# Storing linear-attention features as split parts: the step is moved from the output pairs to the down projection

## The chip, the cores and the metric

The kernel runs on 1 core of a Trainium2 chip. The metric is the device time of one execution in microseconds (us); the time before is the median of three runs. Names of engines follow the profile: PE (TensorE matmul), PEld (its weight loads), DVE (VectorE), ACT (ScalarE), POOL (GpSimd), SP (SyncE, which issues every DMA here).

## The reference

```python
x = A_x                                   # 1 x 2048 x 1024, float32
xn = _layernorm(x, axis=-1)
s = _A_ref(xn, A_wqkv, A_w_phi, A_wo)     # 32 heads of 32, Hedgehog linear attention
g = _silu(_B_ref(xn, B_w_gate, B_w_up, B_w_down))   # (sigmoid(xn Wg) * (xn Wu)) Wd, F = 3584
return x + s * g

# in _A_ref, per head:
pq = q @ w_phi;  pk = k @ w_phi
phi_q = concat(softmax(pq), softmax(-pq));  phi_k = concat(softmax(pk), softmax(-pk))
kv = phi_k^T v;  z = sum over s of phi_k
o = (phi_q kv) / (phi_q z + 1e-6)
return o.reshape(B, S, D) @ wo
```

## The kernel before

Every large product is done in float32 by three TensorE passes: an operand is split into a high part (ACT rounds it to `F32R`) and a low part (DVE subtracts the high part from the source), and `mm3` adds high x high, high x low and low x high (lines 146 to 148). `split` (lines 137 and 138) is the helper for that. On top of it each product is a seven-product Strassen form, with operands named B11, T2, T3, B21, T1, T4, B22.

The stages follow each other: the normalisation and the projections of V, K and Q; the gated products; then the **down stage** (h times `w_down`), and last the **pairs**.

The down stage is a list `dsteps`: for six of the seven operands 14 steps with both token chunks c = 0, 1 (84 steps), then B22 chunk by chunk (28 steps with one chunk). `down_load` issues the DMAs of a step ahead of time (one block of `w_down` or of its sums `wd_d`, and a block of `h_d` for each chunk) into raw half slots from `raw_free`, `down_prep` splits them, one `split` a block, and `mm3` uses them. A tick is one chunk, twelve matmuls. At the end of an operand `evacuate` reads the eight banks out (for B21: a DVE copy, line 1810, and an ACT reload of the bank, line 1811).

In the same ticks `q_late` makes the query features, one unit for each of 16 token tiles t and two halves hb, on a plan of ticks: `weigh` (POOL, line 1005), `density` (DVE, a long reduction and four tiny steps, lines 1010 to 1016), `scale` (POOL, line 1022), `turn` (a DVE transpose, line 1026), `keep` (four DMAs to `et_d`, line 1030). So `et_d` holds the features in float32, divided by the denominator and turned.

The pairs are eight pairs of token tiles. For each, `e_load` (line 1057) fetches the features into slots 47 and 48, one for each q (which half of the k blocks); `phi_part` splits them, `hi` on ACT (line 1070) and `lo` on DVE (line 1072), into the ring `phu`; `numerators` (line 1082, four half-width matmuls) multiplies them by kv; `numerators_out` adds the bank's halves, `cp` on ACT and `ad` on DVE; `o_sum` and `o_part` make the Strassen operands of the next pair; `products` and `product_out` multiply by `wo`; `scaled` (POOL) multiplies by g and adds x; `store` writes the result. `gx_load` fetches g and x.

The order of the pairs is written by hand: `PAIR` is a list of names, and `in_order` ties each engine (PE, DVE, ACT, POOL and SP) to that order. `nm101` means numerators with hb 1, q 0, b 1; `e10` the load for hb 1, q 0; `hi10` and `lo10` its split; `gT20` one k of product T2; `vT2` its read-out; `xT2h` and `xT2l` an operand's split; `m`, `a` the scaling, `l` the load of g and x, `y` the store; `-` and `+` mean the pair before and after. `e` names of hb 1 load for the pair whose numerators run now, `e00+` and `e01+` for the one after. Before the first pair `attend` runs the first numerators between the last steps of the down stage. Elsewhere a scheduler sets the order of the instructions, engine by engine.

Of the kernel before, what the change touches and what calls it, by code (L numbers as in the profile page):

```python
# [50 lines left out]
def hedgehog_glu_kernel(  # L51
# [29 lines left out]
    et_d = dram.tile([TT, 2, P, 2 * HB], F32, name="et_d")  # L81
# [41 lines left out]

    def halves(*ids):
        return [slots[i][:, a] for i in ids for a in range(2)]
# [792 lines left out]

    def down_load():

        n = len(down_loads)
        if nests or len(ops) - 1 not in wraw or n == len(dsteps) or len(raw_free) < 1 + len(dsteps[n][2]):
            return False
        i, j, cs = dsteps[n]
        r, *hr = [raw_free.popleft() for _ in range(1 + len(cs))]
# [3 lines left out]
        down_loads.append((clock[0], r, hr))  # L929
        return True  # L930

    def down_prep():
        n = len(dready)
        if n >= len(down_loads) or not wfree or len(hfree) < len(dsteps[n][2]):
            return False
        at, r, hr = down_loads[n]
        if clock[0] < at + LEAD:
            return False
        w = wfree.popleft()
        split(pair(w), r)  # L940
        hs = {}
# [3 lines left out]
        dready.append((w, hs))  # L945
        for o in (r, *hr):
            down_back(o)
        return True
# [29 lines left out]
    def q_late(at, t, hb):  # L978
# [27 lines left out]

        def density():
            st = hold["sa"] = small.tile([P, 5, 16], F32, name=f"sa{t}{hb}", tag="sa", bufs=2)
            r, d2, r2 = hold["r"], *[st[:, a:a + 2].rearrange("p t h -> p (t h)") for a in (0, 2)]
            nc.vector.tensor_reduce(d2, whole(52).rearrange("p (g d) -> p g d", d=DH), axis=AX.X, op=ALU.add)  # L1010
            nc.vector.tensor_mul(d2, d2, r)
            r, d2, r2 = [a.rearrange("p (b t k) -> p b t k", b=2, t=2) for a in (r, d2, r2)]
            den = st[:, 4].rearrange("p (b k) -> p b k", b=2)
            nc.vector.scalar_tensor_tensor(den, d2[:, :, 0], EPS_DEN, d2[:, :, 1], op0=ALU.add, op1=ALU.add)
            nc.vector.reciprocal(den, den)
            nc.vector.tensor_mul(r2, r, den[:, :, None].to_broadcast([P, 2, 2, 8]))

        def scale():
            e3, r2 = hold["e"].rearrange("p (g d) -> p g d", d=DH), hold["sa"][:, 2:4].rearrange("p t h -> p (t h)")
            for a in range(2):  # L1020
                gs = slice(16 * a, 16 * a + 16)
                nc.gpsimd.tensor_mul(e3[:, gs], e3[:, gs], r2[:, gs, None].to_broadcast([P, 16, DH]))

        def turn():
            hold["et"] = whole(etr.next())
            nc.vector.transpose(hold["et"], hold["e"])

        def keep():
            for c in range(4):
                nc.sync.dma_start(et_d[t, hb, c * DH:(c + 1) * DH].rearrange("f (a x) -> a f x", a=4),  # L1030
                                  hold["et"][:, c * 256:(c + 1) * 256])
# [3 lines left out]
        for n, f in steps + ((11, weigh), (14, density), (15, scale), (18, turn), (18, keep)):  # L1035
            later(at + n, f)
# [7 lines left out]
    phu = Ring((44, 20))  # L1044
# [3 lines left out]
    e_next, units_ph, of = {(u, q): 0 for u in range(2) for q in range(2)}, {}, {}  # L1048
# [5 lines left out]
    def e_load(u, q):  # L1054
        tp_, hb = divmod(e_next[u, q], 2)
        if tp_ < NTP:
            nc.sync.dma_start(slots[47 + q][:, u].rearrange("p (a x) -> p a x", a=4),
                              et_d[2 * tp_ + u, hb].rearrange("p (a q x) -> p q a x", a=4, q=2)[:, q])
        e_next[u, q] += 1

    nbank = {}

    def phi_part(part, hb, q):
        if part == "hi":
            b = run(phu.next(), 2).rearrange("p a b n -> p (a b n)")
            units_ph[hb, q] = b.rearrange("p (a k t) -> p a k t", a=2, t=256)
        hi, lo = [units_ph[hb, q][:, a].rearrange("p k (c t) -> p k c t", t=32) for a in range(2)]
        src = whole(47 + q).rearrange("p (c k t) -> p k c t", k=4, t=32)
        if part == "hi":
            nc.scalar.copy(hi, src)  # L1070
        else:
            nc.vector.tensor_sub(lo, src, hi.bitcast(F32))  # L1072

    def numerators(hb, q, b):

        ph = units_ph[hb, q]
        kg = slots[KVB[hb]][:, q].rearrange("p (k m) -> p k m", m=P)
        nbank[hb, q, b] = ps = nmr.next()
        for j in range(2):
            k = 2 * j + b  # L1080
            for a in range(2):
                nc.tensor.matmul(ps[:, j * 256:(j + 1) * 256], kg[:, k], ph[:, a, k], start=a == 0, stop=a == 1)
# [14 lines left out]

    def o_part(tp_, i, part):
        (b11, b12), (b21, b22) = [(o[:, 0], o[:, 1]) for o in oraw]
        b = {B11: b11, T1: b11, B22: b22, T2: b22, T3: b12, B21: b21, T4: b21}[i]  # L1100
        if tp_ not in of:
            of[tp_] = {j: ofr.next() for j in range(7)}
# [6 lines left out]
    def attend():  # L1109

        def phi(hb, q):
            for part in ("hi", "lo"):
                phi_part(part, hb, q)
            for u in range(2):
                e_load(u, q)
# [5 lines left out]
        def numerator(hb, q):  # L1121
# [4 lines left out]
            if (hb, q) == (0, 1):  # L1126
                of[0] = {i: ofr.next() for i in range(7)}
                o_operand(B11)
                o_sum("s11")
# [6 lines left out]
        for hb in range(2):  # L1136
            ph, nm = [[(f, hb, q) for q in range(2)] for f in (phi, numerator)]

            out += [*ph, *nm]
# [693 lines left out]
    for n, (i, j, cs) in enumerate(dsteps):  # L1833
# [30 lines left out]
        if n == ND - 2 * NJ:  # L1864
            assert len(WO[B21]) == 4
            side.extend([lambda k=k: wo_prep(B21, k) for k in range(4)])
            side.extend([lambda u=u, q=q: e_load(u, q) for q in range(2) for u in range(2)])
        if n == ND - NJ:
# [5 lines left out]
            step(1000)  # L1874
            side.extend([lambda fn=fn, a=a: fn(*a) for fn, *a in attend()])
# [29 lines left out]
    for n in range(2):  # L1905
# [7 lines left out]
        gB110 mT4- xT4h- gB111 vB22- xT4l- gB112 mT1- hi00 gB113 gT20 lo00 aT1- e10 gT21 hi01 aT4- vB11 gT22 lo01 e11 gT23  # L1913
        lB22- gB210 lB21- nm001 cp001 yT1- nm000 yT4- cp000 ad001 gB211 vT2 ad000 gB212 nm011 cp011 ad011 hi10 gB213 mB22-
        nm010 lo10 e00+ w0 w1 aB22- gT30 w2 w3 cp010 ad010 hi11 vB21 gT31 nm101 lT1- yB22- cp101 lo11 e01+ gT32 aB21 ad101
        xB11h nm100 gT33 cp100 yB21 gT10 xB11l nm111 lT4 ad100 s11 cp111 vT3 gT11 nm110 ad111 cp110 xT1h ad110 gT12 xT1l
        gT13 xB22h sA xB21h gT40 vT1 gT41 xB22l xT3h gT42 xB21l sB gT43 xT3l gB220 gB221 sC xT2h gB222 vT4 gB223
        xT2l""".split()
# [70 lines left out]
    def last_weights(k):  # L1989
# [9 lines left out]
        (r"(hi|lo)(\d)(\d)", True, lambda p, part, h, q: phi_part(part, int(h), int(q))),  # L1999
# [6 lines left out]
        (r"e(\d)(\d)", True, lambda p, h, q: [e_load(u, int(q)) for u in range(2) if e_next[u, int(q)] == 2 * p + 2 + int(h)]),  # L2006
# [51 lines left out]
```

## Time and profile before

| what | value |
|---|---|
| median of three runs | 2352.37 us (2348.41 to 2358.05) |
| the profiled execution | 2348.29 us, span 2346.5 us |
| PE busy | 2307.9 us, 98% of the span |
| DVE, ACT, POOL busy | 1750.8, 1231.1, 1153.2 us |
| mean granted TensorE clock | 0.943 |
| DMA | 631.33 MB, 269 GB/s mean |
| stores to `et_d` | 1635.4 to 2054.0 us after the start |
| loads from `et_d` | 1977.9 to 2304.4 us |

A row of the timeline gives start, duration, engine, line, operation and tiles, and in square brackets how long the engine stood idle before it and what ended that. A row of the waits gives the waiting engine and line, the releaser, total us, how often, and the longest. A matmul's duration is modelled and overlaps the next one's, so the distance of starts is what counts. A row of a group gives the busy time, the mean in ns, and the idle time before it. The granted clock is a share of full speed; 0.95 is what the profile shows where PE is busy without a gap.

### The profile page before, as it was taken

Reading aid. Unit: us, or ns where it says so; the run is one execution under the profiler, and the core shown is the slowest. Engines: PE = TensorE matmul, PEld = TensorE weight load, DVE = VectorE, ACT = ScalarE, POOL = GpSimd, SP = SyncE. Lnnn points to the kernel's source line nnn. Section 1 sums busy time; section 2 is a strip of 40 time slices with the busy share of each in tenths; the row PEclk is TensorE's granted clock in tenths of the full one; section 3 lists DMA queues with packets and bytes.
Section 4 is the critical chain, followed back from the end, with each engine's and each line's share of the span. In section 5 each row is a group of like instructions: output and inputs, shape, how many; then the busy total and the mean of one; then the engine's idle time right before and its main releaser. Section 6 shows DMA issues by size and latency. Waiting matters only on the chain.

```text
span 2346.5 us, 32121 instructions
## 1 busy us (share of the span) xinstructions
PE 2307.9 (98%) x10533; PEld 1918.4 (82%) x10533; DVE 1750.8 (75%) x2107; ACT 1231.1 (52%) x1965; POOL 1153.2 (49%) x813
## 2 busy tenths in 40 slices
PE   9999999999999999999999999999989999998988
PEld 8888888888888888888888888888878888877777
DVE  8625777876888774777874665657999999977887
ACT  7354577776555555555555545444444345354543
POOL 1323436772231054665653666764464445424676
PEclk9999999999999999999999999999989999989989
DMA  8789977988778868897886867679767666786665
GB/s 298 267 308 364 333 288 286 354 305 311 273 263 296 274 241 281 302 310 265 286 309 222 293 216 246 224 274 352 255 227 241 232 208 217 268 278 218 197 202 178
DMA packets 344185, 631.33 MB, mean 269 GB/s; under 512 B 37841, under 2 KB 87249, under 8 KB 339409
## 3 DMA queue, kind: packets, MB, share of 16 engines
q1 hardware_dynamic: 344016, 629.28, 77.8%
q8 instruction: 82, 1.34, 0.2%
q14 instruction: 87, 0.70, 0.1%
HBM read 378.34 MB, written 250.81 MB: 268 GB/s over the span
## 4 chain that ended last, share of the span: by engine, by line
PE 85%; DVE 6%; DMA 5%; issue 2%; SPq 1%; ACT 1%; POOL 1%; DVEq 0%; ACTq 0%; POOLq 0%
PE bank L147 27%; PE bank L148 27%; PE bank L146 27%; DMA fc<-g_d 2%; PE bank L381 1%; PE bank L744 1%; DMA fa<-h_d 1%; DVE x L1072 1%; DVE x L1107 1%; DVE fb L1072 1%; DMA et_d<-x 1%; DVE w L138 1%; DMA fa<-w_down 0%; DVE x L138 0%; DMA fc<-et_d 0%
## 5 line engine op out<-in xcount | busy, mean ns | idle before, releaser
L146 PE MATMUL bank<-x,w 128*128 128x512 f32 x2248 | 875.1, 390 | 9.9 <-ACT bank L1811 7.5
L147 PE MATMUL bank<-x,w 128*128 128x512 f32 x2248 | 876.7, 390 | 4.9 <-DVE x L138 4.9
L148 PE MATMUL bank<-x,w 128*128 128x512 f32 x2248 | 875.6, 390 | 0.0
L138 DVE TENSOR_TENSOR w<-fa,w 128x512 fp32r<-128x512 f32 (+2 forms) x394 | 395.0, 1009 | 259.0 <-ACT w L137 246.8
L146 PEld LDWEIGHTS bank<-x,w 128*128 128x128 f32 x2248 | 423.1, 188 | 98.7 <-ACT bank L1811 7.9
L147 PEld LDWEIGHTS bank<-x,w 128*128 128x128 f32 x2248 | 423.2, 188 | 93.0 <-DVE x L138 6.1
L148 PEld LDWEIGHTS bank<-x,w 128*128 128x128 f32 x2248 | 422.9, 188 | 87.9
L137 ACT CAST w<-fa 128x512 fp32r<-128x512 f32 (+2 forms) x394 | 267.9, 684 | 318.9 <-PE bank L147 201.4
L146 PE MATMUL bank<-w,x 128*128 128x512 f32 x708 | 278.3, 393 | 0.0
L148 PE MATMUL bank<-w,x 128*128 128x512 f32 x708 | 276.5, 391 | 0.0
L147 PE MATMUL bank<-w,x 128*128 128x512 f32 x708 | 276.4, 390 | 0.0
L148 PEld LDWEIGHTS bank<-w,x 128*128 128x128 f32 x708 | 133.4, 188 | 28.5 <-DVE x L1256 0.7
L146 PEld LDWEIGHTS bank<-w,x 128*128 128x128 f32 x708 | 133.6, 189 | 26.3
L147 PEld LDWEIGHTS bank<-w,x 128*128 128x128 f32 x708 | 133.7, 189 | 26.2
L138 DVE TENSOR_TENSOR w<-fb,w 128x512 fp32r<-128x512 f32 (+1 forms) x116 | 113.8, 983 | 40.3 <-ACT w L137 40.1
L137 ACT CAST w<-fb 128x512 fp32r<-128x512 f32 (+1 forms) x116 | 70.4, 607 | 108.5 <-PE bank L147 80.8
L138 DVE TENSOR_TENSOR x<-fb,x 128x512 fp32r<-128x512 f32 (+1 forms) x87 | 88.7, 1022 | 19.0 <-ACT x L137 16.0
L1401 ACT COPY fc<-bank 128x512 f32<-128x512 f32 x116 | 66.7, 583 | 39.0 <-PE bank L148 15.6
L138 DVE TENSOR_TENSOR p<-fc,p 128x512 fp32r<-128x512 f32 (+1 forms) x68 | 54.6, 813 | 38.4 <-ACT p L137 38.1
L137 ACT CAST x<-fb 128x512 fp32r<-128x512 f32 (+1 forms) x87 | 65.3, 753 | 12.2 <-DMA fb<-xr_d 5.5
L686 ACT ACTIVATE fc<-fc 128x1024 f32<-128x1024 f32 x44 | 46.6, 1060 | 45.2 <-DVE fc L683 27.5
L1096 POOL TENSOR_TENSOR fc<-fc 128x512 f32<-128x512 f32 x32 | 50.0, 1564 | 40.9 <-DVE fc L1091 15.1
(411 smaller groups left out, 3815.0 us busy)
## 6 DMA issues: line engine op xcount, KB each, us to landing
m_d<-fc SPq DMA_DIRECT2D x168, 256.0 KB
fa<-h_d SPq DMA_DIRECT2D x152, 256.0 KB
fa<-wf_d SPq DMA_DIRECT2D x32, 1024.0 KB
x<-m_d SPq DMA_DIRECT2D x128, 256.0 KB
fa<-w_gu SPq DMA_DIRECT2D x102, 256.0 KB
h_d<-fc SPq DMA_DIRECT2D x102, 256.0 KB
fc<-qkv_d SPq DMA_DIRECT2D x86, 256.0 KB
fb<-w_gu SPq DMA_DIRECT2D x72, 256.0 KB
```

The costliest lines, as they stand in the source:

```text
L137: nc.scalar.copy(o[0], src)
L138: i = nc.vector.tensor_sub(o[1], src, o[0].bitcast(F32))
L146: nc.tensor.matmul(o, a[0], b[0], start=first, stop=False, **kw)
L147: nc.tensor.matmul(o, a[0], b[1], start=False, stop=False, **kw)
L148: last_mm[:] = [nc.tensor.matmul(o, a[1], b[0], start=False, stop=last, **kw).ins]
L381: nc.tensor.matmul(ps[:, gs], r[:, gs], bd[:, 4 * f + g], start=g == 0, stop=g == 3, skip_group_check=True)
L686: nc.scalar.activation(e, e, AF.Exp)
L744: nc.tensor.matmul(kvb[g // 2][:, g % 2 * 256:g % 2 * 256 + 256], v[:, g].rearrange("p a f -> p (a f)"), ph[:, g].rearrange("p a f -> p (a ...
L1072: nc.vector.tensor_sub(lo, src, hi.bitcast(F32))
L1096: nc.gpsimd.tensor_sub(o, a, b)
L1107: nc.vector.tensor_sub(lo, b, hi.bitcast(F32))
L1401: nc.scalar.copy(o, banks[b])
```

## The change

**In the down stage** a unit of features now ends with its split. `density` keeps only the long reduction on DVE; three tiny steps become `denominators` on POOL, the reciprocal stays on DVE as `inverse`, and the last tiny product goes to POOL at the head of `scale`. After `turn` comes `parted`: ACT casts the high part, DVE subtracts in place. `keep` stores both parts, eight DMAs in place of four, and `et_d` is twice as large. Each later step of a unit stands two to five ticks later.

**Down's raw blocks**: where a step has both chunks, `raw_take` finds a whole slot for the two blocks of h, one DMA fetches them and one `split` of 1024 columns a partition makes both.

**In the pairs** `phi_part` and the slots 47 and 48 are gone. `e_load` fetches both parts, four DMAs for a q, into slots 44, 45 (q 0) and 20, 21 (q 1), and the numerators read those slots. There is one such buffer for a q. `PAIR` is written anew, and the operands of the next pair take their slots in another order.

```diff
-        for c, o in zip(cs, hr):
-            nc.sync.dma_start(o, h_d[i, j, :, c])
+        if slot is None:
+            nc.sync.dma_start(hr[0], h_d[i, j, :, cs[0]])
+        else:
+            nc.sync.dma_start(slots[slot], h_d[i, j])
...
-        for c, o in zip(dsteps[n][2], hr):
-            hs[c] = hfree.popleft()
-            last_split[:] = [split(pair(hs[c]), o).ins]
+        if slot is None:
+            i = split(pair(hs[0]), hr[0])
+        else:
+            o = run(hs[0], 2)
+            i = split((o[:, :, 0], o[:, :, 1]), slots[slot])
...
             nc.vector.tensor_reduce(d2, whole(52).rearrange("p (g d) -> p g d", d=DH), axis=AX.X, op=ALU.add)
-            nc.vector.tensor_mul(d2, d2, r)
-            nc.vector.scalar_tensor_tensor(den, d2[:, :, 0], EPS_DEN, d2[:, :, 1], op0=ALU.add, op1=ALU.add)
+        def denominators():
+            r, d2, _, den = parts()
+            nc.gpsimd.tensor_mul(d2, d2, r)
+            nc.gpsimd.tensor_add(den, d2[:, :, 0], d2[:, :, 1])
+            nc.gpsimd.tensor_scalar_add(den, den, EPS_DEN)
+        def inverse():
             nc.vector.reciprocal(den, den)
-            nc.vector.tensor_mul(r2, r, den[:, :, None].to_broadcast([P, 2, 2, 8]))
         def scale():
+            nc.gpsimd.tensor_mul(r2, r, den[:, :, None].to_broadcast([P, 2, 2, 8]))
...
+        def parted():
+            nc.scalar.copy(hold["hi"].bitcast(F32R), hold["lo"])
+            nc.vector.tensor_sub(hold["lo"].bitcast(F32R), hold["lo"], hold["hi"])
...
-        for n, f in steps + ((11, weigh), (14, density), (15, scale), (18, turn), (18, keep)):
+        for n, f in steps + ((11, weigh), (14, density), (15, denominators), (16, inverse), (17, scale), (20, turn),
+                                  (21, parted), (23, keep)):
...
+    def e_load(q):
+        tp_, hb = divmod(e_next[q], 2)
         if tp_ < NTP:
+            for a in range(2):
+                for u in range(2):
+                    o = slots[e_slots[q] + a][:, u].bitcast(F32)
+                    nc.sync.dma_start(o.rearrange("p (a x) -> p a x", a=4),
+                                      et_d[2 * tp_ + u, hb, a].rearrange("p (a q x) -> p q a x", a=4, q=2)[:, q])
+        e_next[q] += 1
...
-                nc.tensor.matmul(ps[:, j * 256:(j + 1) * 256], kg[:, k], ph[:, a, k], start=a == 0, stop=a == 1)
+                nc.tensor.matmul(ps[:, j * 256:(j + 1) * 256], kg[:, k], ph[a][:, :, k], start=a == 0, stop=a == 1)
...
-        gB110 mT4- xT4h- gB111 vB22- xT4l- gB112 mT1- hi00 gB113 gT20 lo00 aT1- e10 gT21 hi01 aT4- vB11 gT22 lo01 e11 gT23
+        gB110 mT1- vB22- aT1- lB22- gB111 nm001 cp001 mT4- gB112 nm000 e10 ad001 cp000 aT4- lB21- yT1- gB113 vB11 gT20 nm011
+        ad000 cp011 mB22- yT4- gT21 nm010 e11 ad011 cp010 aB22- lT1- gT22 ad010 yB22- gT23 xB11h vT2 w0 w1 nm101 xB11l cp101
```

SP in one middle pair, before. `fc<-et_d` are the loads of features (e10 and e11 at first, two DMAs each), `g_d` and `x` the loads of g and x, `out` the stores.

```order
L1057 DMA fc_101<-et_d 128x4x128 x4
L1902 DMA fc_101<-g_d 128x512
L1903 DMA fc_101<-x 128x512
L1902 DMA fc_101<-g_d 128x512
L1903 DMA fc_101<-x 128x512
L1967 DMA out<-fb_0_99 128x512
L1967 DMA out<-p_3_16248 128x512
L1057 DMA fc_101<-et_d 128x4x128 x2
```

The same stretch of SP after. `fb` is the buffer of q 0 (slots 44, 45), `x_4` that of q 1 (slots 20, 21); the first row is e10, the second load row e11.

```order
L1116 DMA fb_15910<-et_d 128x4x128 x4
L1946 DMA fc_101<-g_d 128x512
L1947 DMA fc_101<-x 128x512
L2010 DMA out<-fb_0_99 128x512
L2010 DMA out<-p_3_16224 128x512
L1116 DMA x_4_15908<-et_d 128x4x128 x4
L1946 DMA fc_101<-g_d 128x512
L1947 DMA fc_101<-x 128x512
L2010 DMA out<-fb_0_99 128x512
L1116 DMA fb_15910<-et_d 128x4x128 x4
```

Both e10 and e11 are four DMAs now; between them stand a g and an x load and two stores, which before stood behind both.

PE in the middle of a pair, before: numerators nm001, nm000 on `fb` (the split of q 0), then products, and nm011 on `x_4` (that of q 1).

```order
L1082 MATMUL bank_102<-fb_15942,p_9711 128x256 x4
L1082 MATMUL bank_103<-fb_15942,p_9711 128x256 x4
L146 MATMUL bank_106<-w_95,x_7_15941 128x512
L147 MATMUL bank_106<-w_95,x_7_15941 128x512
L148 MATMUL bank_106<-w_95,x_7_15941 128x512
L146 MATMUL bank_106<-w_95,x_7_15941 128x512
L147 MATMUL bank_106<-w_95,x_7_15941 128x512
L148 MATMUL bank_106<-w_95,x_7_15941 128x512
L1082 MATMUL bank_104<-x_4_15940,p_9711 128x256 x4
```

PE after, from nm010 (the last that reads q 1's first half) to nm101 (the first that reads what e10 fetched).

```order
L1128 MATMUL bank_105<-x_4_15908,p_9711 128x256 x4
L150 MATMUL bank_107<-x_5_11981,fa_16223 128x512
L151 MATMUL bank_107<-x_5_11981,fa_16223 128x512
L152 MATMUL bank_107<-x_5_11981,fa_16223 128x512
L150 MATMUL bank_107<-x_5_11981,fa_16223 128x512
L151 MATMUL bank_107<-x_5_11981,fa_16223 128x512
L152 MATMUL bank_107<-x_5_11981,fa_16223 128x512
L1128 MATMUL bank_102<-fb_15910,p_9711 128x256 x4
```

The numerators moved towards the pair's start: the first two stand behind the products gB111 and gB112 (before: behind gB210), and the two that read what e10 and e11 fetch follow the last reader of the same buffer at a distance of five products and two numerators.

DVE in the down stage, before, around one unit's `density` (L1010 to L1016) with down's splits (L138) between.

```order
L1010 TENSOR_REDUCE sa_13480<-fc_101 128x32
L138 TENSOR_TENSOR x_2_5913<-fa_98,x_2_5913 128x512
L1011 TENSOR_TENSOR sa_13480<-sa_13480,stq_13280 128x32
L1026 STREAM_TRANSPOSE x_3_9793<-x_6_12000 128x1024
L138 TENSOR_TENSOR w_95<-fa_98,w_95 128x512
L1014 SCALAR_TENSOR_TENSOR sa_13480<-sa_13480 128x16
L1015 RECIPROCAL sa_13480<-sa_13480 128x16
L1016 TENSOR_TENSOR sa_13480<-stq_13280,sa_13480 128x32
```

DVE after, one unit's reduction (L1053) and reciprocal (L1063), with another unit's transpose (L1075) and its subtraction of the high part (L1079); a split (L142) of 128x2x512 is one of two blocks.

```order
L1053 TENSOR_REDUCE sa_14458<-fc_101 128x32
L142 TENSOR_TENSOR x_2_5913<-fb_100,x_2_5913 128x512
L142 TENSOR_TENSOR w_95<-fa_98,w_95 128x2x512
L1075 STREAM_TRANSPOSE x_3_9793<-fc_101 128x1024
L695 TENSOR_REDUCE stq_14373<-x_6_11984 128x32
L142 TENSOR_TENSOR x_2_5913<-fb_0_99,x_2_5913 128x512
L1063 RECIPROCAL sa_14458<-sa_14458 128x16
L696 RECIPROCAL stq_14373<-stq_14373 128x32
L1079 TENSOR_TENSOR x_3_9793<-x_3_9793 128x1024
```

The three tiny products are gone from DVE, and the reciprocal stands behind work of POOL.

More of the change, by code (lines that the diff above doesn't have):

```diff
@@ L1047, in hedgehog_glu_kernel @@
     nmr, amm = Ring(banks[:4]), Ring(banks[4:])
[L1048 removed]
+    e_next, of, e_slots = [0, 0], {}, (44, 20)
     oraw = [slots[50], slots[51]]
@@ L1101, in o_part @@
         if tp_ not in of:
-            of[tp_] = {j: ofr.next() for j in range(7)}
+            operands_of(tp_)
         hi, lo = pair(of[tp_][i])
@@ L1126, in numerator @@
             if (hb, q) == (0, 1):
-                of[0] = {i: ofr.next() for i in range(7)}
+                operands_of(0)
                 o_operand(B11)
@@ L1136, in attend @@
         for hb in range(2):
-            ph, nm = [[(f, hb, q) for q in range(2)] for f in (phi, numerator)]
-            out += [*ph, *nm]
+            out += [(int,)] * 6
+            for q in range(2):
+                out += [(numerator, hb, q), (e_load, q)]
         return out
```

111 lines of the change are left out of this document (63 added, 48 removed).

## The prediction

> **What bounds the kernel now.** I read the page first, then the table by windows, PE's waits, and then the chain of waits and the timelines of the last 215 us, where the waits lie.
>
> ```profile
> span 2346.5 us, 32121 instructions
> ...
> PE 2307.9 (98%) x10533; PEld 1918.4 (82%) x10533; DVE 1750.8 (75%) x2107; ACT 1231.1 (52%) x1965; POOL 1153.2 (49%) x813
> ...
> PE 85%; DVE 6%; DMA 5%; issue 2%; SPq 1%; ACT 1%; POOL 1%; DVEq 0%; ACTq 0%; POOLq 0%
> ```
>
> The profiled execution took 2348.3 us, 1.8 beyond its span and 4.1 below the median of the three runs (2352.4). TensorE carries the chain. What can be won is its idle time alone.
>
> ```profile
> 1700.00:1750.00 50.00, 42.53 (x179) 34.69 (x178) 45.57 (x60) 21.70 (x36) 28.33 (x20) 0.89 0.70 232
> 1900.00:1950.00 50.00, 50.00 (x223) 41.39 (x222) 47.41 (x64) 18.72 (x30) 24.33 (x18) 0.95 0.67 211
> 2200.00:2250.00 50.00, 45.09 (x207) 37.47 (x206) 43.72 (x45) 24.25 (x37) 37.36 (x22) 0.89 0.58 187
> ...
> PE bank L1082 <- DVE x L1072: 10.6, 6, 2.4
> PE bank L146 <- ACT bank L1811: 7.5, 1, 7.5
> PE bank L147 <- DVE x L138: 4.9, 3, 2.5
> PE bank L146 <- DMA x<-wo_d: 3.6, 4, 1.3
> ...
> PE bank L1082 <- DVE fb L1072: 2.8, 7, 0.8
> PE bank L146 <- ACT x L137: 2.4, 1, 2.4
> ```
>
> Columns of the windows: length, then PE, PEld, DVE, ACT, POOL busy, granted clock, DMA share, GB/s. At 1900 (down stage) PE has no gap, though DVE is busy for 47.41 of 50. Nearly all waits of PE lie at three places: 7.5 us at 1736 (banks read out at the end of B21), 7.3 at the end of the down stage (L147, L137), and in the pairs, at the numerators (L1082), which wait for the feature split's low part (L1072).
>
> ```profile
> 2029.73 0.39 PE L147 MATMUL bank<-x,w 128*128 128x512 f32 x1
> ...
> 2051.03 0.39 PE L148 MATMUL bank<-x,w 128*128 128x512 f32 x1
> ...
> 2139.68 1.11 PE L1082 MATMUL bank<-fb,p 128*128 128x256 f32 x8
> 2168.01 1.12 PE L1082 MATMUL bank<-fb,p 128*128 128x256 f32 x8
> 2302.99 1.11 PE L1082 MATMUL bank<-fb,p 128*128 128x256 f32 x8
> 2204.26 0.62 PE L1082 MATMUL bank<-x,p 128*128 128x256 f32 x3 [2.22 <-DVE x L1072]
> ...
> 2201.50:2204.91 3.41, 1.19 (x7) 0.84 (x6) 3.20 (x3) 1.18 (x2) 3.33 (x3) 0.95 1.07 333
> 2204.92:2208.33 3.41, 3.41 (x11) 2.85 (x10) 3.29 (x6) 1.68 (x3) 1.71 (x2) 0.50 1.01 327
> 2312.14:2315.55 3.41, 1.79 (x12) 1.55 (x12) 3.32 (x5) 0.58 (x1) 2.78 (x2) 0.95 0.69 216
> 2315.56:2318.96 3.40, 3.40 (x16) 2.63 (x16) 3.34 (x6) 1.88 (x4) 1.86 (x2) 0.95 0.84 283
> ```
>
> 95 matmuls stand from 2029.73 to 2051.03: 0.2266 us each. Eight half-width ones take 1.11 with the last one's modelled 0.28, so 0.12 each. A pair has 84 and 32 of them: 19.0 + 3.8 = 22.9 us. Each pair's first numerators start at 2139.68, 2168.01 (28.3 later) and, five pairs on, at 2302.99: 27.0 each. So 4.1 us of a pair are lost: about 2.5 to waits, and the rest to the clock. The 2.22 us wait left PE 1.19 busy in one 3.41 us window, and the next window ran at 0.50, with 11 matmuls for 16; with 1.79 busy the clock stayed at 0.95.
>
> **The change part by part.** *Pairs, what goes.* Four casts on ACT and four subtractions on DVE (L1070, L1072) leave each pair, so 13.4 us of PE waits (10.6 + 2.8) and their slow windows go. What is late next is the load: a numerator now reads the DMA's own target, one buffer for each q, so the load for the second half (e10, e11) can start only when the first half's numerators are done, and PE waits for it directly. There are four 256 KB loads where there were two.
>
> ```profile
> 2218.92 3.42 SPq L1057 DMA_DIRECT2D fc<-et_d  x4
> 2223.52 5.89 DMA fc<-g_d
> GB/s 0 0 0 0 0 0 0 0 2 170 217 285 266 320 309 309 193 39 164 188 238 295 311 313 285 324 217 193 180 139 66 98 131 98 188 287 344 303 295 328
> ...
> 2097.71 1.20 SPq L1057 DMA_DIRECT2D fc<-et_d  x2
> 2104.12 1.05 ACT L1070 CAST fb<-fc 128x1024 fp32r<-128x1024 f32 x1 [2.88 <-DMA fc<-et_d]
> ```
>
> The GB/s row is 2218 to 2228 in slices of 0.25 us. The first bytes come 1.3 us after the issue at 2218.92, and two loads (0.52 MB) are through by 2222.25: 1.0 us a load. So four land 5.3 us after the first issue in an empty queue at best; in a full one, two needed 6.4 (2097.71 to 2104.12). Only the two loads of lB22 stand shortly ahead of e10, so I take 5.8. Between the last numerator of q=0's first half and the first of its second half, PE has five products and two numerators: 15 x 0.2266 + 8 x 0.12 = 4.4 us. First wait: 1.4 us (ends 0.9 and 4).
>
> e11 stands on SP behind e10, a g and an x load (lB21) and two stores: 12 transfers. At best 1.3 + 8 x 1.0 + 4 x 0.8 (256 KB at 330 GB/s) = 12.5 us after e10's issue. The worst from rows: four loads and three others took from 2218.92 to 2229.41 (the chain's piece, 2223.52 + 5.89), 10.5 us; with one more and four loads, 15.3. PE comes to that numerator after 4.4 + 1.4 + two numerators and three products (3.0) = 8.8. Second wait: 3.7 to 6.5; I take 4.0, near the low end, as the high one holds a lull (the GB/s row's 66 to 139). A wait of 4 us leaves some window under 1.2 us busy, so a slow window follows; it costs (1 - 11/16) x 3.41 = 1.1, less what of it falls into the wait: 1.0 (ends 0 and 1.6). A pair then takes 22.9 + 1.4 + 4.0 + 1.0 = 29.3, +2.3 in each of five. In the first pair there is nothing to store or fetch between e10 and e11, so the second wait is 1.3 + 8.0 - 8.8 = 0.5; and the loads w0 to w3 now stand ahead of e00, so the 3.6 us for wo_d go: 24.8 for 28.3, -3.5. The last stretch, from 2302.99 on: 1.6 of waits go (the window at 2312.14), 6.4 come: +4.8. Sum for the pairs 11.5 - 3.5 + 4.8 = +12.8 (ends -3 and +30).
>
> The numerators' right operand is now read in pieces of 32 columns, 128 apart. No matmul here shows that: between nothing and twice 0.12 x 32, or +3.8 a pair. ACT's cast at 2104.12 read the same tile in the same pieces, 1.05 us for 1024 columns, so I take nothing.
>
> The Trainium skill (TensorE: Matmul & The Clock Gate, What's actually happening) lets the clock fall after at least one idle window of about 3.4 us; by that a 4 us wait seldom fills an aligned window, and the sum would be 6 us lower. The trace differs: a 2.22 us wait was enough.
>
> *End of the down stage.*
>
> ```profile
> 2062.05 1.04 ACT L1070 CAST x<-fc 128x1024 fp32r<-128x1024 f32 x1 [9.45 <-DMA fb<-w_down]
> 2064.98:2068.38 3.40, 0.92 (x3) 0.51 (x3) 3.40 (x3) 3.40 (x8) 2.95 (x3) 0.50 0.76 236
> ```
>
> ACT stood 9.45 us before a feature cast, with down's splits queued behind; that made PE's 4.9 and 2.4 and about 2.5 more at clock 0.50. The cast is gone, and PE itself waits for the loads at the first numerators, in a full queue, for 0 to 10: -5 (ends -9 and +2).
>
> *Down stage.*
>
> ```profile
> L138 DVE TENSOR_TENSOR w<-fa,w 128x512 fp32r<-128x512 f32 x131 | 121.6, 936 | 19.1 <-ACT w L137 17.8 <-issue 1.0 <-PE bank L148 0.3
> L1011 DVE TENSOR_TENSOR sa<-sa,stq 128x32 f32<-128x32 f32 x20 | 16.2, 809 | 0.0
> L1014 DVE SCALAR_TENSOR_TENSOR sa<-sa 128x16 f32<-128x16 f32 x32 | 11.5, 360 | 0.4
> L1016 DVE TENSOR_TENSOR sa<-stq,sa 128x32 f32<-128x32 f32 x20 | 6.0, 298 | 0.5
> L138 DVE TENSOR_TENSOR w<-fa,w 128x1024 fp32r<-128x1024 f32 x66 | 92.0, 1401 | 86.2 <-ACT w L137 86.0
> L534 POOL TENSOR_TENSOR fa<-fa 128x256 f32<-128x256 f32 x7 | 5.2, 738 | 50.3 <-DMA fa<-wg_d 46.4 <-DVE bank L1579 3.9
> 1705.85 0.68 DVE L138 TENSOR_TENSOR w<-fb,w 128x512 fp32r<-128x512 f32 x1
> 1706.44 1.78 DVE L138 TENSOR_TENSOR x<-fb,x 128x512 fp32r<-128x512 f32 x1
> 1718.24 1.25 DVE L1026 STREAM_TRANSPOSE x<-x 128x1024 f32<-128x1024 f32 x1 [3.21 <-POOL x L1022]
> 1736.27 0.79 PE L146 MATMUL bank<-x,w 128*128 128x512 f32 x1 [7.47 <-ACT bank L1811]
> L1030 SPq DMA_DIRECT2D et_d<-x x128: 503/514/1444, 1635.4 to 2054.0; - x128
> ```
>
> DVE: the tiny steps leave, 32 x (0.81 + 0.36 + 0.30) = -47 us; 84 block pairs split as one, 84 x (1.40 - 2 x 0.94) = -40; 32 feature subtractions come, x 1.40 = +45. Together -42: DVE gets room, but PE has no gap there, so 0. ACT gains 32 casts of 1.05 and loses 84 starts; it is busy for 18.7 to 21.7 of 50. POOL gets 128 tiny steps: from nothing to the 0.74 of the smallest row, and up to 1.1 of waiting for DVE (a split takes 1.78 beside POOL, 0.68 alone); at 0.6 each 77 us in the 419 us from 1635.4 to 2054.0, so some 35 of 50 busy. A unit's chain now crosses between DVE and POOL twice more, and DVE stands in order (3.21 at the transpose). Splits queue behind, and PE behind them; cover is the splits made ahead. +1 (0 to +12). SP: 128 more stores x 0.51, or +66 us of issue in those 419, less 84 loads, and 16.8 MB more to write beside a DMA share of 0.67; the loads are issued steps ahead: 0.
>
> *The 7.47 us at 1736.* DVE comes late to the read-out, with the same work queued ahead: 0 (ends -9 and +3).
>
> Sum: 12.8 - 5 + 0 + 1 + 0 = +8.8 on 2348.3, or 2357.1; with the 4.1 to the median, 2361.
>
> **The rivals.** *Loads that come nearly in time, on the other side* (0.15): with waits of 0.5 and 2.0 and no slow window a pair takes 25.4: 5 x -1.6, -3.5 in the first, +0.9 in the last, -5 before them: about 2337. It decides below 4.1 us lost in a pair. For it: DVE, the bound of the pairs, loses four of its longest steps. Against it: 5.3 us at best against 4.4, and 16 loads x 1.0 and 12 other transfers x 0.8 are 25.6 us of queue in each pair. *POOL's steps starve the splits* (0.20): DVE waits for the reciprocal's operand behind POOL's 128x512 steps, and PE loses one or two more stretches like 1736's (7.5 and a slow window, 9 each): 2370 to 2380. For it 47.41 of 50, against it the -42 us. The Trainium skill (Perfetto Trace Analysis, Optimizing Scalar/DVE Operations) says that moving work between VectorE and GpSimd might not help, since they share a port; the 1.78 beside 0.68 agrees. *The read-out's wait goes* (0.15): DVE's room removes the 7.47 and its slow window: 2352, no change.
>
> **How the numbers follow.** My case has 0.50, at 2352 to 2372. 0.5% (11.8 us) is about what a measurement can tell. Slower: some 0.20 of my case, nearly all of POOL's rival and a rest, 0.41; faster: most of the first rival and a rest, 0.15; within, 0.44. The 8 in 10 range reaches from the first rival (2338) to POOL's (2381); the likeliest case's own is 2352 to 2372.
>
> **What would show it.** Right: no L1070 or L1072; PE waits at L1128 for DMA et_d, twice in a pair, 1 to 2 and 3.5 to 6 us; first numerators 29 us apart; clock 0.50 once in a pair; DMA share over 0.75 in the pairs; PE at 50 of 50 in the down stage with DVE near 43. Wrong: numerators 23 to 26 us apart, or gaps of PE between 1640 and 2040 other than that at the end of B21.

## The result, and the profile after

The changed kernel takes 2500.3 us (median of 4, 2498.6 to 2501.3) beside 2351.9 for the kernel before on the same chip: 1.063 times as long, 95% interval 1.060 to 1.065. The forecast was 2361. The profiled execution took 2500.8, 1.8 more than its span. Line numbers from here on are the changed kernel's unless another kernel is named: L150 to L152 are `mm3`, L141 and L142 `split`, L1075 the transpose, L1078 and L1079 the new split of the features, L1084 the stores of `keep`, L1128 the numerators.

The page, its first lines and the chain that ended last by engine:

```profile
span 2499.0 us, 31982 instructions
...
PE 2354.3 (94%) x10533; PEld 1938.6 (78%) x10533; DVE 1676.8 (67%) x1927; ACT 1217.1 (49%) x1881; POOL 1213.9 (49%) x941
...
PE 66%; DMA 16%; DVE 6%; SPq 4%; POOL 3%; issue 3%; ACT 1%; DVEq 0%; ACTq 0%; POOLq 0%
```

PE has fallen from 85% of the chain to 66%, DMA has risen from 5% to 16% and SP's queue from 1% to 4%. DVE is less busy than before (67% for 75%), ACT too, and POOL has gained only 61 us in the whole run: nothing that computes has become the bound.

The same three windows as in the prediction (length, PE, PEld, DVE, ACT, POOL busy, granted clock, DMA share, GB/s):

```profile
1700.00:1750.00 50.00, 35.80 (x132) 28.00 (x131) 34.54 (x38) 15.38 (x19) 27.29 (x26) 0.83 0.59 205
1900.00:1950.00 50.00, 37.59 (x137) 29.26 (x136) 33.50 (x38) 19.86 (x28) 24.82 (x25) 0.84 0.57 199
2200.00:2250.00 50.00, 39.29 (x166) 32.05 (x167) 28.28 (x41) 24.09 (x43) 8.63 (x6) 0.86 0.97 317
```

At 1900 PE did 223 matmuls before and 137 now, and the DMA share went *down*, from 0.67 to 0.57, although each unit has more to move. (The clock columns compare only within one profile: without a gap, the one before shows 0.95 at 223 matmuls in 50 us, the later ones 1.00 at 222 or 223.) The whole stretch from 1700 to 2100 us:

```profile
1700.00:2100.00 400.00, 331.66 (x1332) 264.30 (x1330) 281.24 (x304) 154.38 (x199) 217.10 (x203) 0.91 0.61 210
```

PE is idle for 68 of these 400 us. Its matmuls take 0.249 us each of the busy time, where 0.2266 is the pace without a gap; that makes another 30 us, the price of the lower clock behind the gaps.

To place the loss, I set the two traces side by side at equal numbers of matmuls (both have all 10533). The table gives what each stretch takes beyond the kernel before, worked out from the starts of those matmuls; its times count from the first matmul, 1.5 us into the span. The other columns are experiments told below.

| stretch, by matmul (time before) | changed | wide | late2 | bdouble |
|---|---|---|---|---|
| up to 7800 (1699.5 us) | +0.7 | +1.3 | -1.1 | +6.0 |
| 7800 to 9200, down stage (2026.6) | +93.3 | -3.6 | -2.7 | +96.1 |
| 9200 to 9600, its end and the first numerators (2124.4) | +27.6 | -10.2 | -9.2 | +29.1 |
| 9600 to the end, pairs | +31.1 | +29.7 | +5.9 | +0.2 |

Of the 153 us, 121 are lost before the pairs begin: 93 where the forecast had written +1, and 28 where it had -5. PE's largest wait between 1640 and 2130 us (us in total, times, longest):

```profile
PE bank L151 <- DVE x L142: 47.4, 17, 8.6
```

ACT's waits in the same stretch:

```profile
ACT x L1078 <- DVE x L1075: 144.0, 22, 12.0
ACT w L141 <- DMA fa<-h_d: 37.1, 11, 6.1
ACT x L141 <- DMA fb<-wd_d: 34.7, 11, 9.6
```

And DVE's largest:

```profile
DVE x L1075 <- DMA et_d<-x: 35.4, 9, 8.9
```

PE waits for splits. The largest number, ACT's 144 us before the features' cast, invites a wrong reading: that an in-order ACT stands at the new cast for a late transpose, with down's splits behind it. The last three rows say what ends those waits: loads of h and wd that come late, and transposes that wait for a *store* to read its slot out. The chain of waits over one such stretch, in order of time (start, length, what; pieces under 0.1 us left out):

```profile
1756.52 1.34 SPq L1084
...
1757.90 1.72 SPq L1084
...
1759.67 8.19 DMA et_d<-x
...
1767.92 8.36 DMA fa<-h_d
...
1776.30 6.70 DMA et_d<-x
```

Store, load, store, each 6.7 to 8.4 us from issue to landing. What the transfers do meanwhile, in three windows of 2 us (the last two columns are DMA share and GB/s):

```profile
1758.00:1760.00 2.00, 2.00 (x10) 1.67 (x9) 2.00 (x4) 2.00 (x5) 1.79 (x2) 1.00 0.27 97
1762.00:1764.00 2.00, 2.00 (x10) 1.65 (x10) 0.00 (x0) 0.61 (x1) 2.00 (x3) 1.00 0.27 97
1766.00:1768.00 2.00, 2.00 (x11) 1.65 (x10) 1.02 (x1) 2.00 (x5) 2.00 (x2) 1.00 0.97 293
```

And the DMA view from 1759 to 1765:

```profile
DMA packets 565, 0.58 MB, mean 96 GB/s; under 512 B 20, under 2 KB 545, under 8 KB 565
...
q1 hardware_dynamic: 565, 0.58, 27.1%
```

This is the reading that the case turns on. For several us on end the share stands at 0.27 and the rate at 96 GB/s: 0.27 x 16 is 4.3, so about four of the 16 DMA engines work and twelve are idle. The trace's single packets say so too: at any moment from 1759.5 to 1765 four to six of them were in flight, and from 1752 to 1754 sixteen or more. A store of 128 KB then takes 131072 / 96e3 = 1.36 us, and a unit's eight take 10.9 us out of the 13.1 us that a unit had before (32 units in the 419 us from 1635.4 to 2054.0).

The stores hold up the rest at SP, which issues in order. What it does at that time (start, length, and how many; L951 and L955 issue the loads of a coming down step):

```profile
1755.22 8.54 SPq L1084 DMA_DIRECT2D et_d<-x  x7
1763.87 1.60 SPq L951 DMA_DIRECT2D fb<-wd_d  x1
1765.52 0.43 SPq L955 DMA_DIRECT2D fa<-h_d  x1
```

For 8.54 us SP stands at seven stores, 1.2 us each, and the next load is issued only then. The twelve engines are idle because no load has reached them: with the loads issued, the share is 0.97 from 1766 to 1768, while the stores' packets go on at the same rate beside them. An issue of a store took 0.51 us at the median before and takes twice that now. The stores' line, with the shortest, median and longest issue in ns:

```profile
L1084 SPq DMA_DIRECT2D et_d<-x x256: 502/1058/3582, 1646.7 to 2194.6; - x128
```

The store writes `f (a x) -> a f x`: the DRAM side's outermost size is a = 4. The Trainium skill (DMA: Bandwidth & Descriptors, Why a DMA increments its semaphore by 16 and not by 1) says that a transfer is split over the largest k up to 16 that divides the outermost sizes of both its sides; with 128 partitions and 4 that is 4. The trace's 0.27 agrees.

### The profile page after: what moved, and what is told of

The parts are those of the page before. It is cut to its first block, busy times and chain, and to the rows that moved or that the text cites. A ratio compares the mean times of both kernels' runs of the same rounds, so it can differ in the third digit from the quotient of the medians.

```text
span 2499.0 us, 31982 instructions
## 1 busy us (share of the span) xinstructions
PE 2354.3 (94%) x10533; PEld 1938.6 (78%) x10533; DVE 1676.8 (67%) x1927; ACT 1217.1 (49%) x1881; POOL 1213.9 (49%) x941
## 4 chain that ended last, share of the span: by engine, by line
PE 66%; DMA 16%; DVE 6%; SPq 4%; POOL 3%; issue 3%; ACT 1%; DVEq 0%; ACTq 0%; POOLq 0%
PE bank L150 21%; PE bank L152 21%; PE bank L151 21%; DMA et_d<-x 4%; DMA fa<-h_d 2%; SPq L1084 2%; DVE w L142 2%; DMA x<-et_d 1%; DMA x<-e_d 1%; PE bank L385 1%; PE bank L748 1%; SPq L1116 1%; POOL fc L1142 1%; DMA fc<-qkv_d 1%; DMA fb<-et_d 1%
## 5 line engine op out<-in xcount | busy, mean ns | idle before, releaser
L151 PE MATMUL bank<-x,w 128*128 128x512 f32 x2248 | 891.5, 397 | 48.0 <-DVE x L142 47.9
L150 PE MATMUL bank<-x,w 128*128 128x512 f32 x2248 | 887.4, 396 | 41.1 <-ACT x L141 9.2
L152 PE MATMUL bank<-x,w 128*128 128x512 f32 x2248 | 884.6, 395 | 4.5 <-DVE w L142 4.5
L142 DVE TENSOR_TENSOR w<-fa,w 128x512 fp32r<-128x512 f32 (+2 forms) x344 | 392.9, 1146 | 276.8 <-ACT w L141 271.5
L151 PEld LDWEIGHTS bank<-x,w 128*128 128x128 f32 x2248 | 430.3, 191 | 146.7 <-DVE x L142 58.3
L150 PEld LDWEIGHTS bank<-x,w 128*128 128x128 f32 x2248 | 430.0, 191 | 135.9 <-ACT x L141 10.0
L152 PEld LDWEIGHTS bank<-x,w 128*128 128x128 f32 x2248 | 430.1, 191 | 95.1 <-DVE w L142 5.6
L141 ACT CAST w<-fa 128x512 fp32r<-128x512 f32 (+2 forms) x344 | 272.6, 795 | 266.0 <-PE bank L151 108.6
L150 PE MATMUL bank<-w,x 128*128 128x512 f32 x704 | 277.3, 394 | 0.0
L152 PE MATMUL bank<-w,x 128*128 128x512 f32 x704 | 276.2, 392 | 0.0
L152 PEld LDWEIGHTS bank<-w,x 128*128 128x128 f32 x704 | 133.2, 189 | 28.6 <-DVE x L1299 1.1
L150 PEld LDWEIGHTS bank<-w,x 128*128 128x128 f32 x704 | 133.4, 189 | 26.3
L142 DVE TENSOR_TENSOR x<-fb,x 128x512 fp32r<-128x512 f32 (+1 forms) x121 | 120.9, 1002 | 25.7 <-ACT x L141 22.8
L1078 ACT CAST x<-x 128x1024 fp32r<-128x1024 f32 x32 | 33.5, 1048 | 171.7 <-DVE x L1075 148.4
L141 ACT CAST x<-fb 128x512 fp32r<-128x512 f32 (+1 forms) x121 | 86.4, 716 | 63.0 <-DMA fb<-wd_d 34.7
L142 DVE TENSOR_TENSOR w<-fb,w 128x512 fp32r<-128x512 f32 (+2 forms) x82 | 84.3, 1028 | 40.7 <-ACT w L141 40.4
L1137 DVE TENSOR_TENSOR fc<-fc,bank 64x512 f32<-64x512 f32 x64 | 43.8, 685 | 86.0 <-ACT fc L1135 85.8
L1135 ACT COPY fc<-bank 64x512 f32<-64x512 f32 x64 | 37.2, 582 | 108.0 <-PE bank L1128 107.7
L142 DVE TENSOR_TENSOR p<-fc,p 128x512 fp32r<-128x512 f32 (+1 forms) x68 | 55.6, 828 | 45.8 <-ACT p L141 43.1
```

Source lines behind the costliest of these rows:

```text
L141: nc.scalar.copy(o[0], src)
L142: i = nc.vector.tensor_sub(o[1], src, o[0].bitcast(F32))
L150: nc.tensor.matmul(o, a[0], b[0], start=first, stop=False, **kw)
L151: nc.tensor.matmul(o, a[0], b[1], start=False, stop=False, **kw)
L152: last_mm[:] = [nc.tensor.matmul(o, a[1], b[0], start=False, stop=last, **kw).ins]
L1078: nc.scalar.copy(hold["hi"].bitcast(F32R), hold["lo"])
```

## The experiments

Five theories stood at the start. F: the stores run on four of the 16 engines, and what is issued behind them waits. Q: there are simply too many stores for SP, and too many bytes. P: density's tiny steps, handed from DVE to POOL and back, make each unit's chain late. M: a step now waits for a whole free slot, so loads are issued late. A: ACT stands in order at the new cast. For the pairs there is E: PE waits for the loads into the one buffer of each q.

**wide** keeps bytes, packets and the number of stores, and writes the same data with f = 32 outermost:

```diff
-                for c in range(4):
-                    nc.sync.dma_start(et_d[t, hb, a, c * DH:(c + 1) * DH].rearrange("f (a x) -> a f x", a=4),
-                                      hold[part][:, c * 256:(c + 1) * 256])
+                for a in range(4):
+                    nc.sync.dma_start(et_d[t, hb, n].rearrange("(c f) (a x) -> a f c x", c=4, a=4)[a],
+                                      hold[part][a * DH:(a + 1) * DH].rearrange("f (c x) -> f c x", c=4))
```

> The changed kernel, with each part of a unit stored in four pieces of 32 partitions (one for each a, written as f, c, x) in place of four pieces written as a, f, x. Bytes, number of stores and 1 KB packets stay. Theory F (a store whose outermost size is 4 runs on four of the 16 DMA engines, 1.36 us each at 96 GB/s with the DMA share at 0.27, and all that is issued later stands behind it): the stretches at 0.27 go, issues of the store fall from 1.04 to about 0.5 us, the down stage gets back 90 to 120 us, total 2380 to 2410. Theory Q (the number of stores on SP and their bytes): 2490 to 2500, as now. Theories P (POOL's tiny steps) and M (blocks loaded as one): 2480 to 2500.

Measured: 2365.3 us (1.006 times before, interval 1.004 to 1.009). 135 us are back, more than F had asked for. (The edit also changes what a piece reads, 32 partitions in place of 128. No run separates the two; the share of the engines and the packets in flight speak for the outermost size.) Its page:

```profile
span 2363.4 us, 31993 instructions
...
PE 86%; DMA 4%; DVE 4%; POOL 2%; issue 1%; SPq 1%; ACT 1%; DVEq 0%; POOLq 0%; ACTq 0%
```

The stores' line and a window of the down stage:

```profile
L1084 SPq DMA_DIRECT2D et_d<-x x256: 302/439/1591, 1647.3 to 2064.6; - x128
```

```profile
1900.00:1950.00 50.00, 50.00 (x222) 41.43 (x221) 45.32 (x47) 21.92 (x27) 33.02 (x32) 1.00 0.84 265
```

PE's only wait of more than 1.5 us before 2060, and then ACT's at the cast, from 1640 to 2130:

```profile
PE bank L150 <- ACT bank L1854: 4.1, 1, 4.1
```

```profile
ACT x L1078 <- DVE x L1075: 55.2, 17, 8.9
```

From the read-out near 1730 to 2100 us PE has no gap. ACT still stands 55 us at the cast for the transpose, up to 8.9 us at a time, and PE does not notice: theory A falls here, as does the large number as a sign. So P and M, left as they are in this kernel, cost nothing that PE sees either. Added up, SP stands at the 256 issues for 265 us in the changed kernel and for 123 in wide. From the first store to the last, three to seven packets were in flight for 0.51 of the time in the changed kernel, 0.26 in the one before and 0.03 in wide.

**half** leaves out the four stores of each unit's low part. Bytes and number halve as well, so it cannot tell F from Q.

```diff
-            for a, part in enumerate(("hi", "lo")):
+            for a, part in enumerate(("hi",)):
...
-                                      et_d[2 * tp_ + u, hb, a].rearrange("p (a q x) -> p q a x", a=4, q=2)[:, q])
+                                      et_d[2 * tp_ + u, hb, 0].rearrange("p (a q x) -> p q a x", a=4, q=2)[:, q])
```

> The changed kernel without the four stores of each unit's low part; the pairs read the high part for both, so the output lacks the low parts. Cast, subtraction and loads in the pairs stay. F: half of the four-engine time goes, 5.4 us of 10.9 in a unit: most of the loss in the down stage goes, 2390 to 2420. Q: the same, as stores and bytes halve too (this run tells F and Q from P and M, not from one another). P and M: 2480 to 2500. A (ACT stands in order before the cast for the transpose): 2480 to 2500 if the transpose is late by itself.

Measured: 2372.7 us; its stretch from 7800 to 9200 takes 2.8 less than before's. It falls below its range: F had expected some of the loss to stay. The loss is far from in proportion: up to the pairs, half, with four narrow stores in a unit (5.4 us), takes 8 us more than wide, with all of it at the end of the down stage, and the changed kernel, with eight, 134 more. SP's issue gives a reason, though no run tests it alone: in half its median is 0.52 us, so four stores seldom make SP stand.

**dve** puts density's tiny steps back on DVE (first cut); **unmerge** brings back the two h blocks loaded and split one by one (second cut).

```diff
-            nc.gpsimd.tensor_mul(d2, d2, r)
-            nc.gpsimd.tensor_add(den, d2[:, :, 0], d2[:, :, 1])
-            nc.gpsimd.tensor_scalar_add(den, den, EPS_DEN)
...
+            nc.vector.tensor_mul(d2, d2, r)
...
+            nc.vector.scalar_tensor_tensor(den, d2[:, :, 0], EPS_DEN, d2[:, :, 1], op0=ALU.add, op1=ALU.add)
...
```

```diff
-            nc.sync.dma_start(slots[slot], h_d[i, j])
...
+        for c, o in zip(cs, hr):
+            nc.sync.dma_start(o, h_d[i, j, :, c])
```

> The changed kernel with density's tiny steps back on DVE (the five steps as before, in one go; big scale step at its place in the changed kernel). P: the two handovers to POOL and back go and the transposes come early: 2380 to 2420. F, Q and M: 2485 to 2505.

> The changed kernel with the two h blocks of a down step loaded and split one by one, as before. M (a step waits for a whole free slot, so loads are issued late): 2380 to 2420. F, Q and P: 2480 to 2510, a little more on DVE and ACT.

Measured: 2502.1 and 2501.0 us. Neither P nor M carries the loss. Alone these two would not prove that they cost nothing, since the stores' wait could cover a smaller one; wide shows that.

**bdouble** adds the suspected cost, and nothing else, to the kernel before: each narrow store is issued twice.

```diff
-            for c in range(4):
-                nc.sync.dma_start(et_d[t, hb, c * DH:(c + 1) * DH].rearrange("f (a x) -> a f x", a=4),
-                                  hold["et"][:, c * 256:(c + 1) * 256])
+            for o in (et_d, et2_d):
+                for c in range(4):
+                    nc.sync.dma_start(o[t, hb, c * DH:(c + 1) * DH].rearrange("f (a x) -> a f x", a=4),
+                                      hold["et"][:, c * 256:(c + 1) * 256])
```

> The kernel before with each unit's four stores issued twice, the second time into a second tensor that nobody reads. No cast, no second slot, no new order: the four-engine time alone is doubled, to 10.9 us in a unit. F: most of the changed kernel's loss in the down stage comes back, 2430 to 2480. If the doubled stores need the changed kernel's fuller ring or ACT's in-order cast as well: 2355 to 2400.

Measured: 2478.8 us, 1.054 times before (1.052 to 1.056): +127. PE's largest wait from 1640 to 2140 (in its own line numbers: L148 and L139 are `mm3` and `split`):

```profile
PE bank L148 <- DVE x L139: 54.8, 15, 8.4
```

Its down stage from 1700 to 2100 us, PE busy for 333 of 400 us at a DMA share of 0.61:

```profile
1700.00:2100.00 400.00, 333.14 (x1346) 267.47 (x1345) 287.24 (x411) 140.18 (x230) 155.14 (x112) 0.91 0.61 208
```

Without the cast, the second slot, the new order or any further step on POOL, the loss in the down stage comes back whole (+96 and +29 in the table's two middle rows). Adding narrow stores is enough to make it, and widening them enough to remove it.

**many** cuts the wide pieces again, into 16 partitions: 16 stores in a unit, outermost size still 16.

```diff
+                    for f in (0, 16):
+                        nc.sync.dma_start(et_d[t, hb, n].rearrange("(c f) (a x) -> a f c x", c=4, a=4)[a, f:f + 16],
+                                          hold[part][a * DH + f:a * DH + f + 16].rearrange("f (c x) -> f c x", c=4))
```

> The changed kernel with each part stored in eight pieces of 16 partitions, written as f, c, x: 16 stores of 64 KB in a unit where the changed kernel has 8 of 128 KB, the same bytes and 1 KB packets, an outermost size of 16. F (stores on four engines): 2362 to 2380, as with four wide pieces for each part. Q (the number of stores that SP issues): worse than the changed kernel, 2510 to 2600, since SP has 256 stores more to issue. Against F would also be anything over 2420.

Measured: 2402.2 us, between the two. Up to the pairs it loses 23 us on the kernel before. The DMA view from 1789.5 to 1792, while such stores run, and then wide's from 2034.25 to 2036.5, where its stores run alone:

```profile
DMA packets 492, 0.42 MB, mean 168 GB/s; under 512 B 96, under 2 KB 477, under 8 KB 492
...
q1 hardware_dynamic: 492, 0.42, 80.4%
```

```profile
DMA packets 755, 0.69 MB, mean 305 GB/s; under 512 B 85, under 2 KB 755, under 8 KB 755
...
q1 hardware_dynamic: 755, 0.69, 98.1%
```

The share is 0.80, but the bytes come at 168 GB/s, little more than half of wide's 305 (256 in another such stretch, from 1956.5 to 1958.5). SP stands at the 512 issues for 220 us in all. So twice as many stores as the changed kernel has do not bring its loss, and Q falls as its cause; but F's range was missed as well: the share of engines is not the whole rate. Whether the 16 partitions that each piece reads or SP's 256 further issues made the 37 us over wide is open.

**bwide** gives the kernel before the wide stores.

> The kernel before with its stores in the wide form (f, c, x), else as it was. F: its 5.4 us on four engines in a unit were covered but for single waits; so at most the 7.3 us at the end of the down stage and a few more go: 2340 to 2353. More than 20 us would mean that the stores had cost before what no wait of PE shows.

Measured: 2343.6 us, 0.9966 times before (0.9953 to 0.9979): within the range, most of it (-6.7) at the end of the down stage. That is nearly the 8 us by which half and wide differ there: four narrow stores in a unit cost 7 to 8 us in either kernel.

**late** and **late2** take the wide stores and move the second half's numerators back in the pairs' order, so that the loads issued at `e10` and `e11` have longer. The core of late2's order as a diff against the changed kernel's, lines joined:

```diff
- xB11h vT2 w0 w1 nm101 xB11l cp101 gB210 w2 w3 nm100 e00+ s11 ad101 cp100 gB211 gB212 ad100 nm111 cp111 gB213 xT1h nm110 e01+
+ xB11h vT2 w0 w1 xB11l s11 gB210 w2 w3 gB211 xT1h gB212 xT1l gB213 vB21 gT30 nm101 cp101 aB21 lT4 gT31 nm100 e00+ ad101 cp100
+ gT32 ad100 yB21 gT33 vT3 gT10 gT11 nm111 cp111 gT12 nm110 e01+
```

> The changed kernel with wide stores, and the pairs' order written anew in one point: the four numerators of the second half (nm101 to nm110) and what follows from them stand five products later, so that the loads issued at e10 and e11 have 4 to 6 us more; the first half's loads have as much less, of some 15. Theory E (PE waits for the one buffer's loads, 4 to 5 us in a pair, and for the slow clock behind it): a pair falls from 31.2 to 27 or 28 us, total 2335 to 2348. If the pairs are bound by the loads' volume (a share of 0.80): 2360 to 2370, with the waits at the first half's numerators. If by DVE's or ACT's chain behind the numerators: 2365 to 2390.

> The changed kernel with wide stores, and the second half's numerators moved further: q=0 two products behind where the first try had them, q=1 four, with what follows from them. Products between a load's issue and its first reader, by the order: first half 16 and 13, second half 10 and 12, where the first try had 18, 17, 8 and 8. Theory E (PE waits for the one buffer's loads): the waits of 2.2 and 1.4 us that the first try left at q=1 go, a pair falls from 29.3 to 26 or 27 us, total 2328 to 2340, below both kernels. Volume (the loads fill the queue, share 0.84 in the pairs): 2346 to 2352, the waits turn up at the first half. A chain behind the late numerators (xT2 and xT4 come too late for the next pair's products): above 2352, with waits at the products of T2 or T4.

Measured: late 2351.2 (0.9999 times before, 0.9989 to 1.0009), late2 2341.9 (0.9962, 0.9948 to 0.9976). PE's waits at the numerators, first of wide over the whole run, then of late from 2060 on, then of late2 from 1640 on:

```profile
PE bank L1128 <- DMA fb<-et_d: 21.1, 9, 3.8
PE bank L1128 <- DMA x<-et_d: 13.3, 9, 2.3
```

```profile
PE bank L1128 <- DMA x<-et_d: 18.9, 13, 2.5
PE bank L1128 <- DMA fb<-et_d: 8.1, 9, 3.0
```

```profile
PE bank L1128 <- DMA fb<-et_d: 14.7, 10, 2.0
PE bank L1128 <- DMA x<-et_d: 6.0, 7, 1.3
```

The waits fall from 34.4 to 27.0 and 20.7 us. E holds, but both runs came in a little above its range, since waits of up to 2 us stay; with a DMA share of 0.86 in late2's pairs, the loads' volume may be the next limit, which no run tests. late2 beats the kernel before and the changed one by its interval; bwide and late2, 1.7 us apart, were timed in different sets and are not told apart.

## Why the prediction was wrong, point by point

**The step that failed: "SP: 128 more stores ... the loads are issued steps ahead: 0."** It priced a store by the 0.51 us of its issue and by its bytes beside a mean DMA share of 0.67. Neither is what a narrow store costs. It occupies four engines for 1.36 us. With several in a row SP's next issue takes about as long, the loads behind it are issued late, and the steps issued ahead did not cover 10.9 us in every 13. Its size is what lies between the changed kernel and wide: 97 us in the down stage and 38 at its end. The fact stood in the trace of before, in a view that the prediction did not use, the transfers while the stores run (share of the engines in tenths and GB/s, 1755.5 to 1760 us in 40 slices):

```profile
DMA  5654922322222322232497579999746799977453
GB/s 182 228 164 182 273 64 55 73 55 73 73 64 82 100 82 91 91 109 91 146 237 164 164 264 328 391 410 382 264 155 237 264 373 373 428 291 282 155 118 91
```

Some 1.5 us at a share of 0.2 to 0.3, with other transfers before and behind. A mean share of 0.67 hides it: three to seven packets were in flight for 0.26 of the time between the first store and the last, so by estimate 0.26 x (1 - 0.27) = 0.19 of the unused 0.33 was engines that a transfer did not reach, and not room.

**Down stage otherwise: +1 for POOL's chain and 0 for DVE and ACT.** By wide -3.6 with the read-out: right. The rival of POOL's steps falls (dve changed nothing; in wide PE has no gap). My list of what would show it wrong, "gaps of PE between 1640 and 2040", named the sign, but no rival had this mechanism.

**The read-out near 1736: 0.** The wait there is 4.1 in wide for 7.47; the stretch's -3.6 is mostly this. Within the ends given (-9 and +3).

**End of the down stage: -5 (-9 to +2).** In wide -10.2 together with the first numerators: right in sign, a little beyond the end. The loads of the first numerators came in time there.

**Pairs: +12.8; measured +31.1**, just beyond the upper end of 30. The mechanism was right, one buffer for each q and PE waiting twice in a pair; its two waits and the clock were mis-sized. First numerators of three pairs of the changed kernel (the first, the second and the seventh):

```profile
2256.66 0.64 PE L1128 MATMUL bank<-fb,p 128*128 128x256 f32 x4
2290.57 0.64 PE L1128 MATMUL bank<-fb,p 128*128 128x256 f32 x4
2445.43 0.64 PE L1128 MATMUL bank<-fb,p 128*128 128x256 f32 x4
```

Its waits at L1128 in the five pairs from 2290.5 to 2445.4, and two windows behind such a wait:

```profile
PE bank L1128 <- DMA fb<-et_d: 14.6, 6, 3.6
PE bank L1128 <- DMA x<-et_d: 8.0, 8, 1.3
```

```profile
2361.72:2365.13 3.41, 3.41 (x12) 3.02 (x13) 0.69 (x1) 1.05 (x2) 0.00 (x0) 0.50 1.11 362
2365.14:2368.55 3.41, 2.83 (x10) 1.97 (x10) 0.68 (x1) 0.10 (x1) 0.00 (x0) 0.64 1.09 340
```

Five pairs take (2445.43 - 2290.57) / 5 = 31.0 each, forecast 29.3. The waits are 4.5 of it, forecast 1.4 + 4.0 = 5.4, and that nearness is luck: the first wait (`fb`, q 0) is 2.9 for 1.4, the second (`x`, q 1) 1.6 for 4.0, below its low end of 3.7. PE goes on with what e10 fetched 7.4 to 8.2 us after its issue, where 5.8 was taken, and so comes late to the second wait, which ends 13.3 to 14.3 us after e10's issue, where 12.8 was taken. The rest, 31.0 - 22.9 - 4.5 = 3.6, stood at 1.0 for the clock. Of this, 0.7 is waits at L150 for DVE, which the forecast did not have. For what is left the two windows show one reason: behind this wait the clock was at 0.50 for a whole window and for a part of a second one, where one shortened window was forecast. Another is the price of a window, (1 - 11/16) x 3.41 = 1.1, which counted half-width matmuls as whole ones. Whole ones of the same slow window of before start 0.43 apart, where 0.2266 is the pace:

```profile
2204.95 0.63 PE L147 MATMUL bank<-w,fa 128*128 128x512 f32 x1
2205.38 0.63 PE L148 MATMUL bank<-w,fa 128*128 128x512 f32 x1
```

So it costs (1 - 0.2266/0.43) x 3.41 = 1.6. The five pairs together are 5 x (31.0 - 27.0) = 20 for 11.5. The first pair takes 33.9 for a forecast of 24.8, with waits of 1.4 and 0.5. PE waited 6.1 for what e10 fetched and not at all for e11, and 10 us around and behind these waits ran at half clock at a DMA share of 1.01. The waits from 2256 to 2291, and the slow stretch:

```profile
PE bank L1128 <- DMA fb<-et_d: 6.1, 2, 4.1
```

```profile
2265.20:2275.40 10.20, 6.40 (x19) 5.29 (x20) 1.37 (x2) 1.16 (x2) 0.37 (x1) 0.50 1.01 289
```

With 33.9 - 28.3 = 5.6 for -3.5, this leaves 31.1 - 20 - 5.6 = 5.5 for the two ends of the stretch, where 4.8 stood.

The rival of loads that come nearly in time (0.15) was wrong for this order. With more room for the loads a pair of late2 takes 27.5, between the rival's 25.4 and the 31.0 here, and its pairs' stretch stands at +5.9.

With the stores widened alone, the kernel takes 2365 where 2361 was forecast. That nearness is luck, since there the misses partly cancel: the pairs took 17 more than forecast, the end of the down stage and the read-out 9 less.

## What to carry to other kernels

Price a DMA by the engines that its shape can reach, and not by bytes or its issue: look at the share of DMA in the very slices where transfers of one kind run, and read a flat 0.27 as four engines of 16. Look too at how long the issuing engine stands at them, since what it issues next comes late by that. A mean share well under 1 is no room for more of the same narrow transfer. When PE waits for splits and an engine stands long before one instruction, follow the waits to what ends them, then remove and add the suspected cost alone: here one rewritten access pattern took 135 us away, and the same stores doubled in the old kernel brought 127.

## What the hardware showed that I had not expected

While a row of stores with an outermost size of 4 ran, little else moved: 96 GB/s at a share of 0.27, with SP standing at their issues, 1.06 us at the median where wide ones took 0.44. The step from four to eight such stores in a unit was a cliff: against wide, 8 us in half and 134 in the changed kernel before the pairs. And pieces of 16 partitions moved at 168 GB/s though 0.80 of the engines' time was taken, where 32-partition pieces reached 256 to 305. Behind a wait of PE of 2.2 us, at half the granted clock, matmuls started 0.43 us apart for 0.23.
